# Mixer GEMMs in a seven-product form with four operand sums a side and chained PSUM copies, and x0 normalised ahead of the statistics of x1

## The chip, the cores and the metric

The kernel runs on one core of one Trainium2 chip. The metric is the device time of one execution in microseconds (us), median of the timed runs; lower is better. Three kinds of number appear below and should not be mixed. The *time* of a run (about 578.7 us) covers the whole execution. The *span* (about 577 us) is what the profile of one execution shows from its first to its last instruction. A *start time* such as 236.00 is counted from the beginning of that span.

## The reference, cut to what matters

```python
# A_x [1, 2048, 1024], A_wqkv [1024, 3072], A_wo [1024, 1024]; B_w1 [2048, 3584], B_w2 [3584, 2048]; all bf16
x = A_x
h = x + linear_attention(_layernorm(x), A_wqkv, A_wo)     # 32 heads, phi(t) = elu(t) + 1
def _B_ref(x, w1, b1, w2, b2):                            # the token mixer
    h = _layernorm(x, axis=-1)
    u = jnp.einsum("bsd,sf->bdf", h, w1) + b1             # GEMM 1, contraction over S = 2048
    u = _gelu(u)
    y = jnp.einsum("bdf,fs->bds", u, w2) + b2             # GEMM 2, contraction over F = 3584
    return y.transpose(0, 2, 1)
return h + _B_ref(_layernorm(h), ...)
```

The two mixer GEMMs take 338 of the 577 us. The rest is the first layer norm, the projections, the linear attention, the output projection and the second layer norm.

## The kernel before

The mixer treats each GEMM as a 2x2 block product and does it with seven half-size products in place of eight. GEMM 1 runs 14 "pairs" (two tiles of 128 output rows), with 8 matmuls of 128x512 a product; GEMM 2 runs 8 pairs with 14 matmuls a product. In the class for this, `asum` makes the weight-side operand sums on VectorE, `combine` makes the sums of the moving side on VectorE, and `mK` issues product K and whatever must be done with its result in PSUM.

```python
class Strassen:                       # cut
    self.sa = {3: self.a11, 4: self.a22}
    def asum(self, m):                # five weight-side sums a pair, each on VectorE
        a, b, op = {
            1: (self.a11, self.a22, ALU.add),
            2: (self.a21, self.a22, ALU.add),
            5: (self.a11, self.a12, ALU.add),
            6: (self.a21, self.a11, ALU.subtract),
            7: (self.a12, self.a22, ALU.subtract),
        }[m]
        ...
        return nc.vector.tensor_tensor(t, a, b, op)
    def m2(self, ks=None):            # W = product 2, and a copy of it to SBUF on ScalarE
        ...
        nc.scalar.copy(self.s2[:], self.W[:])
    def m3(self, ks=None):            # Z = product 3;  d = Z - s2                   VectorE
        ...
    def m1(self, ks=None):            # X = product 1;  Y = X + d                    VectorE
        ...
    def m4(self):                     # W += product 4; t = W + d                    VectorE
        ...
    def m5(self, cut=None):           # Z += product 5; t = t - Z;  X = X + t        VectorE, twice
        ...
    def m6(self): ...                 # Y += product 6, evacuate
    def m7(self): ...                 # X += product 7, evacuate (issued within the next pair)
```

The order of a pair in the steady part, and that of the first pair of GEMM 1 (`split`). There the last of the eight matmuls of three products is held back, because the last two row tiles of the layer norm are still being made:

```python
def run_pair(st, nxt, split, pending, cut=None):
    if split:
        for ks in (head, last):
            st.m2(ks); st.m3(ks); st.m1(ks)
        st.m4()
    else:
        st.m2()
        if pending is not None:
            pending.m7()
        st.m3(); st.m4(); st.m1()
    ...  # nxt.asum(2)
    st.m5(cut)
    ...  # nxt.asum(1), nxt.asum(5)
    st.m6()
    ...  # nxt.asum(6), nxt.asum(7)
```

The start of the kernel. `pin` holds an instruction in the written order on its engine. `ln[1][1](c)` is the statistics of half c of row tile x1 (VectorE), `norm_halves(0)` the normalising of x0 (VectorE), and `transpose_in(0)` its eight transposes on TensorE and the copies out of PSUM:

```python
warm_up(10)                     # matmuls on a scratch tile, so that the clock is up
...
ln_stats(0)                     # statistics of x0, VectorE
stats(0)                        # scale of x0: Ln and Exp on ScalarE
ln[1] = ln_chunks(1, xs.pop(1))
pin(ln[1][1](0))                # first half of x1's statistics, VectorE
norm_halves(0)
transpose_in(0)
pin(ln[1][1](1))
pin(ln[1][2]())
stats(1)
k_unit(0, 0)                    # first projection
```

## Time and profile before

| what | measured |
|---|---|
| time, median of 3 runs | 578.66 us (578.49 to 578.73) |
| span of the profile | 577.5 us |
| busy TensorE / VectorE / ScalarE | 569.7 / 385.8 / 212.9 us |
| first mixer matmul starts | 236.00 us |
| last matmul starts | 574.41 us |

In the profile PE is TensorE (matmuls), PEld its weight loads, DVE is VectorE, ACT ScalarE, SPq the queue that issues DMAs. The first view is the line of busy time in the page of the kernel before (busy us, share of the span, instructions):

```profile
PE 569.7 (99%) x2832; PEld 267.3 (46%) x2854; DVE 385.8 (67%) x752; ACT 212.9 (37%) x433; POOL 1.8 (0%) x8
```

A busy matmul engine proves little by itself, because matmuls overlap (each is recorded as 0.379 us long, and the next starts 0.216 us after it) and their ends are modelled. What counts is the pitch from start to start, and whether there are gaps. The next view cuts the mixer of the kernel before into its two GEMMs, and shows for each stretch its length and the busy time and instructions of each engine:

```profile
core 0: us, PE busy (x) PEld busy (x) DVE busy (x) ACT busy (x) POOL busy (x), PEclk, DMA share, GB/s
236.00:406.10 170.10, 170.10 (x790) 77.11 (x789) 115.04 (x204) 48.71 (x75) 0.00 (x0) 1.00 0.30 81
406.10:574.50 168.40, 168.40 (x795) 77.07 (x793) 91.01 (x114) 5.39 (x9) 0.00 (x0) 1.00 0.41 115
```

TensorE is busy for the whole of both stretches. VectorE is busy for two thirds of the first and half of the second and never holds TensorE up. In the chain of work that ended last, one product of eight matmuls takes 1.73 us, so 0.216 us for each matmul (the piece is a whole product of the first pair):

```profile
241.78 1.73 PE psW L228 x8
```

The third view is the timeline of the start of the kernel before (start us, us, engine, line, operation, output <- inputs, shapes, count; in brackets the engine's idle time before it and what ended it):

```profile
3.59 1.29 DVE L396 BATCH_NORM_STATS2 st<-x_sb 128x6 f32<-128x512 bf16 x2 [1.49 <-DMA x_sb<-in_A_x_dram]
...
5.49 0.20 ACT L403 ACTIVATE rstd<-lnv 128x1 f32<-128x1 f32 x1
5.84 0.69 DVE L396 BATCH_NORM_STATS2 st<-x_sb 128x6 f32<-128x512 bf16 x1 [0.72 <-DMA x_sb<-in_A_x_dram]
6.45 0.72 DVE L406 TENSOR_SCALAR xn<-x_sb,mv,rstd 128x512 bf16<-128x512 bf16 x2
...
6.91 0.72 PE L670 MATMUL tp<-ident,xn 128*128 128x128 bf16 x8 [1.26 <-DVE xn L406]
```

The scale of x0 (`rstd`) is ready at 5.69 us, the end of the ACTIVATE. VectorE then does a half of x1's statistics, normalises x0 from 6.45 on, and x0's transposes start at 6.91.

### The profile page before, as it was taken

The page shows a single profiled execution, that of the slowest core. Times are in us where ns is not written, and L with a number is a line of the kernel's source. Part 1 is how long each engine was busy: PE and PEld are TensorE (multiplying, and loading weights), DVE is VectorE, ACT ScalarE, POOL GpSimd, SP SyncE. Part 2 cuts the span into 40 slices and gives each one's busy share as a digit, 9 for nine tenths or more (in the row PEclk, how much of TensorE's full clock was granted, in tenths as well). Part 3 has the DMA queues.
Part 4 walks back from the last instruction along what each step waited for, and adds up shares of the span by engine and source line. Part 5 has one row for each costly group of instructions (what it writes and reads, how often), then busy time and mean ns, then how long its engine had stood idle before and what let it go on. Part 6 is the DMA issues. An engine that isn't in the chain of part 4 may idle for free.

```text
span 577.5 us, 7489 instructions
## 1 busy us (share of the span) xinstructions
PE 569.7 (99%) x2832; PEld 267.3 (46%) x2854; DVE 385.8 (67%) x752; ACT 212.9 (37%) x433; POOL 1.8 (0%) x8
## 2 busy tenths in 40 slices
PE   7999999999999999999999999999999999999997
PEld 3444444455555444444444444444444444444444
DVE  6898887556767889876756766667765455456443
ACT  4747777656668777332222322223000000000000
POOL 1000000000000000000000000000000000000000
PEclk9999999999999999999999999999999999999999
DMA  9934431039438952152224322203966446431101
GB/s 304 350 75 77 90 73 37 19 116 273 68 73 176 279 165 92 63 139 73 74 75 122 95 74 73 74 0 95 227 207 161 127 114 173 133 96 47 36 28 36
DMA packets 109827, 66.55 MB, mean 115 GB/s; under 512 B 31826, under 2 KB 101728, under 8 KB 109792
## 3 DMA queue, kind: packets, MB, share of 16 engines
q1 hardware_dynamic: 109056, 65.42, 42.3%
q10 hardware_dynamic: 672, 0.66, 0.4%
q8 instruction: 22, 0.36, 0.3%
q14 instruction: 13, 0.11, 0.1%
q0 software_dynamic: 64, 0.01, 0.0%
HBM read 50.34 MB, written 8.39 MB: 102 GB/s over the span
## 4 chain that ended last, share of the span: by engine, by line
PE 95%; DVE 2%; DMA 1%; issue 1%; SPq 0%; ACT 0%
PE psW L228 17%; PE psZ L228 17%; PE psX L228 17%; PE acc_t L922 10%; PE acc_t L775 9%; PE psY L228 8%; PE psB L503 4%; PE psC L503 4%; PE psA L503 4%; PE psE L503 2%; PE acc_t L427 1%; DMA x_sb<-in_A_x_dram 1%; PE nd_ps L873 1%; DVE wo_sb L477 1%; DVE st L396 0%
## 5 line engine op out<-in xcount | busy, mean ns | idle before, releaser
L228 PEld LDWEIGHTS <-sa 128*128 128x128 f16 x1134 | 110.4, 98 | 131.7
L223 DVE TENSOR_TENSOR sa<-w1p 128x1024 f16<-128x1024 bf16 x70 | 48.0, 686 | 20.0 <-PE psX L228 12.4
L775 PE MATMUL acc_t<-xnT,wq_sb 128*128 128x512 bf16 x248 | 57.3, 379 | 0.4
L922 PE MATMUL acc_t<-wo_sb,pqT 128*128 128x512 bf16 x250 | 55.7, 379 | 0.3
L223 DVE TENSOR_TENSOR sa<-w2p 128x1792 f16<-128x1792 bf16 x40 | 43.4, 1085 | 10.1 <-PE psW L228 7.6
L922 PEld LDWEIGHTS <-pqT 128*128 128x128 bf16 x256 | 24.8, 98 | 29.0
L775 PEld LDWEIGHTS <-wq_sb 128*128 128x128 bf16 x256 | 24.5, 98 | 27.4
L164 DVE TENSOR_SCALAR e_sb<-e_sb 128x512 bf16<-128x512 bf16 x64 | 18.5, 289 | 25.9 <-ACT e_sb L160 25.4
L264 DVE TENSOR_TENSOR tt<-psW,dd 128x512 f32<-128x512 f32 x22 | 15.2, 692 | 29.2 <-PE psW L228 29.2
L228 PEld LDWEIGHTS <-w2p 128*128 128x128 bf16 x224 | 21.9, 98 | 26.4
L228 PEld LDWEIGHTS <-w1p 128*128 128x128 bf16 x224 | 21.9, 98 | 26.4
L259 DVE TENSOR_TENSOR psY<-psX,dd 128x512 f32<-128x512 f32 x22 | 15.4, 700 | 27.5 <-PE psX L228 27.5
L160 ACT ACTIVATE e_sb<-acc_t 128x512 bf16<-128x512 f32 x40 | 23.9, 598 | 26.6 <-PE acc_t L775 23.6
L503 PEld LDWEIGHTS <-xs 128*128 128x128 f16 x208 | 20.1, 98 | 23.3 <-DVE xs L489 1.3
L269 DVE TENSOR_TENSOR tt<-tt,psZ 128x512 f32<-128x512 f32 x22 | 15.1, 688 | 18.0 <-PE psZ L228 17.9
L228 PE MATMUL psZ<-hT_2227,w1p 128*128 128x512 f16 x112 | 26.8, 379 | 0.0
L503 PE MATMUL psA<-wkv,xnT 128*128 128x512 bf16 x98 | 26.4, 379 | 0.3
L228 PE MATMUL psW<-hE,sa 128*128 128x512 f16 x112 | 26.6, 379 | 0.0
L228 PE MATMUL psX<-hT_2226,sa 128*128 128x512 f16 x112 | 26.6, 379 | 0.0
L228 PE MATMUL psX<-hO,sa 128*128 128x512 f16 x112 | 26.5, 379 | 0.0
L228 PE MATMUL psW<-hT_2228,w1p 128*128 128x512 f16 x112 | 26.5, 379 | 0.0
L228 PE MATMUL psZ<-hO,sa 128*128 128x512 f16 x112 | 26.5, 379 | 0.0
(258 smaller groups left out, 840.1 us busy)
## 6 DMA issues: line engine op xcount, KB each, us to landing
w1p<-in_B_w_dram SPq DMA_DIRECT2D x14, 1024.0 KB, 5.7
w2p<-in_B_w_dram SPq DMA_DIRECT2D x8, 1792.0 KB, 8.3
xr<-in_A_x_dram SPq DMA_DIRECT2D x16, 256.0 KB, 3.5
x_sb<-in_A_x_dram SPq DMA_DIRECT2D x15, 256.0 KB, 3.0
wkv<-in_A_wqkv_dram SPq DMA_DIRECT2D x2, 1024.0 KB, 9.2
wq_sb<-in_A_wqkv_dram SPq DMA_DIRECT2D x2, 1024.0 KB, 12.4
wo_sb<-in_A_wo_dram SPq DMA_DIRECT2D x2, 1024.0 KB, 6.4
wkv<-in_A_wqkv_dram SPq DMA_DIRECT2D x3, 512.0 KB, 7.5
```

Of the source, the lines that this page charges most:

```text
L160: pin(nc.scalar.activation(e_sb[:], src, ACT.Exp))
L164: pin(nc.vector.tensor_scalar(e_sb[:], e_sb[:], 1.0, PHI_EPS, ALU.min, ALU.add))
L223: return nc.vector.tensor_tensor(t, a, b, op)
L228: nc.tensor.matmul(ps[:, cols], lhsT=sa[:, k, :], rhs=mv(k)[:, cols], start=(start and k == 0), stop=(stop and k == self.nk - 1), skip_gro ...
L259: nc.vector.tensor_tensor(self.Y[:], self.X[:], self.d[:], ALU.add)
L264: nc.vector.tensor_tensor(self.t[:], self.W[:], self.d[:], ALU.add)
L269: nc.vector.tensor_tensor(self.t[:], self.t[:], self.Z[:], ALU.subtract)
L427: mm = nc.tensor.matmul(pp[:, 0:CW], lhsT=xnT[:, kt, i * P:(i + 1) * P], rhs=wkv[:, kt, c * CW:(c + 1) * CW], start=(kt == 0), stop=(kt == ...
L477: pin(nc.vector.tensor_tensor(out, a, b, ALU.subtract))
L503: pin(nc.tensor.matmul(ps[:], lhsT=lhs[:, k, :], rhs=rhs[:, k, :], start=(start and k == 0), stop=(k == hk2 - 1), skip_group_check=True,))
L775: nc.tensor.matmul(qp[:, 0:SW], lhsT=wq_sb[:, kt, j * P:(j + 1) * P], rhs=xnT[:, kt, u * SW:(u + 1) * SW], start=(kt == 0), stop=(kt == ND ...
L922: nc.tensor.matmul(ap_[:, 0:CW], lhsT=pqT[:, j, i * P:(i + 1) * P], rhs=wo_sb[:, j, dc * CW:(dc + 1) * CW], start=(j == 0 and not SEED_RES ...
```

## The change

The intent is to take work off VectorE. The same seven products a pair are combined in another way: four operand sums a side, some of them built on earlier ones, and accumulators that are chained by copies within PSUM on ScalarE (A to B, B to C), with one shared product E. The last pair of GEMM 1 also prepares the first weight sums of GEMM 2. At the start, x0 is normalised before any statistics of x1.

```diff
-    class Strassen:
+    class Product7:
...
+            self.lhs = {1: self.a11, 2: self.a12, 4: self.a22}
         def asum(self, m):
             a, b, op = {
-                1: (self.a11, self.a22, ALU.add),
-                2: (self.a21, self.a22, ALU.add),
-                5: (self.a11, self.a12, ALU.add),
-                6: (self.a21, self.a11, ALU.subtract),
-                7: (self.a12, self.a22, ALU.subtract),
+                5: (self.a21, self.a22, ALU.add),
+                6: (self.lhs.get(5), self.a11, ALU.subtract),
+                7: (self.a11, self.a21, ALU.subtract),
+                3: (self.a12, self.lhs.get(6), ALU.subtract),
             }[m]
...
+        def p1(self):
+            self.A = psw.tile([P, BANK], F32, tag="w", name="psA1")
+            self.mm(1, self.A, True)
+            self.B = psx.tile([P, BANK], F32, tag="x", name="psB1")
+            nc.scalar.copy(self.B[:], self.A[:])
+        def p5(self, ks=None):        # E = product 5, then shared(E)
+        def p6(self):
+            self.mm(6, self.B, False)
+            self.C = psy.tile([P, BANK], F32, tag="y", name="psC1")
+            nc.scalar.copy(self.C[:], self.B[:])
+        def p2(self, ks=None):        # A += product 2, evacuate
+        def p7(self, cut=None):       # C += product 7, evacuate with E added
+        def p3(self):                 # B += product 3, evacuate with E added
+        def p4(self):                 # C += product 4, evacuate (issued within the next pair)
...
-    def run_pair(st, nxt, split, pending, cut=None):
+    def run_pair(st, nxt, pending, cut=None):
+        st.p1()
+        if pending is None:           # first pair of a GEMM
+            head, last = list(range(st.nk - 1)), [st.nk - 1]
             for ks in (head, last):
+                st.p5(ks)
+                st.p2(ks)
         else:
+            pending.p4()
+            st.p5()
+        st.p6()
+        if pending is not None:
+            st.p2()
+        st.p7(cut)
+        st.p3()                       # asum 5, 6, 7, 3 of the next pair lie between; cut
...
             stats(0)
-            ln[1] = ln_chunks(1, xs.pop(1))
-            pin(ln[1][1](0))
             norm_halves(0)
             transpose_in(0)
-            pin(ln[1][1](1))
-            pin(ln[1][2]())
+            ln_stats(1)
             stats(1)
```

Below, "product 2" and "second product" mean the one with that number (`p2`), not the second in time.

## The prediction

> **What bounds it.** The matmul engine. By the page's first part PE is busy 569.7 of 577.5 us. Busy time alone proves little for pipelined matmuls (the Trainium skill, "Perfetto Trace Analysis", section Identifying the Most-Contended Engine), so I read the pitch. In the chain of waits the mixer is one string of products: 8 matmuls per 1.73 us, 14 per 3.02 us, 0.216 us for a 128x512 matmul. The skill's "TensorE: Matmul & The Clock Gate", section "Wait — 56ns, not 53.3ns?", states 215.7 ns for back-to-back warm ones; the trace agrees. Cut into windows, PE was busy 170.1 of 170.1 us in the first mixer GEMM (236.0 to 406.1) and 168.5 of 168.9 in the second. Most idle PE lies in the first 11 us (1.2 before the warm-up, then 1.3, 0.4, 0.5) and 2.5 us of tail.
>
> **Mixer.** Both forms do seven products per pair with 8 or 14 matmuls each: the same count, so nothing to gain on PE. The load falls elsewhere:
> - VectorE, first GEMM, per pair of 12.1 us: 5 operand sums at 0.69 become 4; 5 PSUM combinations at 0.69 become 2; four 0.42 sums become 3: about 8.6 us becomes 5.4. Second GEMM, per pair of 21.2 us: 5x1.08+5x0.69+4x0.75 = 11.9 becomes 4x1.08+2x0.69+4x0.75 = 8.7.
> - ScalarE: one 0.59 us copy becomes three (two in the second GEMM).
> Off the critical path: worth about 0.
>
> New waits could cost. A product started on a PSUM copy waits for it: 0.2 us until ScalarE sees the last matmul, 0.57 of copy, some 0.05 to PE: 0.85. In the steady order a whole product stands between (1.73 or 3.02), which hides it. In the first pair of each GEMM the built order puts only 5 or 4 matmuls (1.08, 0.86) of the next pair between; in the first GEMM the copy also queues behind the Gelu table load (1.28) and a Gelu (0.69). I give 0 to 0.2 us.
>
> At the hand-over the loads of weight pairs 1 and 2 of the second GEMM now start when the last fourth product ends (406.1), where the first started at 398.5. At the 290 GB/s of those loads before, each takes 6.3 us, and the residual rows behind land near 421.5. VectorE stands still for them, but PE needs its evacuation only at the fourth product, near 427: 2.5 us to spare. This is the thinnest place.
>
> **Start.** Before, after x0's scale was ready (5.69), VectorE did the first statistics of x1 (5.84 to 6.53), and normalising began at 6.45. Now it begins near 5.75: x0's transposes and first projection move 0.7 us ahead. x1's statistics end no later, so x1's transposes, which waited for PE until 9.72, start some 0.4 us earlier. After that PE is continuous to 14.25, and x3's input (landed 12.48) still meets its turn. About 0.35 us should survive to the end.
>
> **Time.** 578.66 - 0.35 + 0.1 of new waits = 578.4 us, 8 in 10 between 577.6 and 579.6. Faster by over 2%: 0.005; within 2%: 0.985; slower: 0.01.
>
> **Right or wrong by.** First transposes near 6.2 instead of 6.9; first mixer matmul near 235.6; mixer windows wholly PE-busy at 0.216 us; VectorE busy down from 386 to about 312, ScalarE up from 213 to about 235; VectorE's long wait for residual rows within 414 to 422, no PE gap after it.
>
> **What would make it wrong.** Residual rows landing after 424 (up to a few us, once); ScalarE's queue order delaying a copy in every pair (0.1 us times 22 would show); the early 0.35 lost to a later DMA landing.

## The result, and the profile after

The changed kernel took 579.02 us (median of 6 runs, 578.84 to 579.42); the kernel before, in runs on the same chip, 578.69 us (6 runs, 578.49 to 580.43). A ratio here is the mean time of one kernel's runs over that of the other's of the same rounds, so it is not quite the ratio of these medians. (Every run here counts, the long ones described below too.) It is 0.9998 (95% interval 0.9983 to 1.0013): the same within 2%, in fact within 0.2%. Both profiled spans are 577.5 us.

The line of busy time in the page of the changed kernel:

```profile
PE 570.2 (99%) x2832; PEld 267.5 (46%) x2854; DVE 323.6 (56%) x641; ACT 234.0 (41%) x470; POOL 1.8 (0%) x8
```

VectorE lost 62 us of work and ScalarE gained 21, with the same number of matmuls. The mixer of the changed kernel in windows, cut at its own hand-over:

```profile
core 0: us, PE busy (x) PEld busy (x) DVE busy (x) ACT busy (x) POOL busy (x), PEclk, DMA share, GB/s
235.57:405.19 169.62, 169.48 (x786) 76.69 (x784) 77.45 (x134) 65.42 (x103) 0.00 (x0) 1.00 0.26 70
405.19:574.50 169.31, 169.31 (x799) 77.48 (x797) 68.02 (x81) 10.06 (x18) 0.00 (x0) 1.00 0.45 125
```

The first stretch has 0.14 us in which TensorE was not busy. Because the ends of matmuls are modelled, I measured gaps from start to start instead: the time by which a matmul starts later than the pitch after the one ahead of it. The kernel before has none above 0.03 us in the whole mixer. The changed kernel has exactly two, both in the first pair of GEMM 1: **0.112 us** before 238.92 and **0.302 us** before 243.96. Its timeline of that pair:

```profile
237.29 1.67 PE L208 MATMUL psE_2922<-hE,sa 128*128 128x512 f16 x7
...
237.85 0.30 ACT L951 ACTIVATE hln_l<-mv_all,eps_85 128x1 f32<-128x1 f32 x1 [1.01 <-DVE mv_all L949]
238.18 0.20 ACT L952 ACTIVATE sc_all<-hln_l 128x1 f32<-128x1 f32 x1
238.29 0.58 ACT L224 COPY psB_2920<-psA_2911 128x512 f32<-128x512 f32 x1
...
238.92 1.67 PE L208 MATMUL psA_2911<-hO,w1p 128*128 128x512 f16 x7
...
240.86 1.89 PE L208 MATMUL psB_2920<-hT_2226,sa 128*128 128x512 f16 x8
241.44 1.28 ACT L272 ACT_TABLE_LOAD   x1
...
242.58 1.24 PE L208 MATMUL psA_2984<-hE,w1p 128*128 128x512 f16 x5
242.74 0.69 ACT L272 ACTIVATE gE<-psA_2911,b_sb 128x512 f16<-128x512 f32 x1
...
243.32 0.59 ACT L236 COPY psC_2952<-psB_2920 128x512 f32<-128x512 f32 x1
...
243.96 0.81 PE L208 MATMUL psC_2952<-hT_2227,sa 128*128 128x512 f16 x3
```

The first gap: product 2 adds to accumulator A (238.92), so the copy from A to B must have *read* A first. That copy, at 238.29, stands in ScalarE's queue behind the scale of the last layer norm (237.85 and 238.18), which itself waited for VectorE. The second gap: product 7 adds to C (243.96), and the copy from B to C stands behind the load of the Gelu table (1.28 us) and the first Gelu (0.69 us). The Trainium skill, "PSUM — Partial Sum Buffer", section Engine vs sequencer instructions, states that the ScalarE queue is a strict first-in, first-out one. The trace agrees: product 6 ended near 242.6 and the copy, due some 0.2 us later, started only at 243.32, while the Gelu ahead of it was finishing.

The timeline of the start of the changed kernel, which answers to that of before:

```profile
5.57 0.20 ACT L421 ACTIVATE rstd<-lnv 128x1 f32<-128x1 f32 x1
5.81 0.74 DVE L424 TENSOR_SCALAR xn<-x_sb,mv,rstd 128x512 bf16<-128x512 bf16 x2 [0.60 <-ACT rstd L421]
6.28 0.95 PE L688 MATMUL tp<-ident,xn 128*128 128x128 bf16 x8 [0.64 <-DVE xn L424]
6.46 1.28 DVE L414 BATCH_NORM_STATS2 st<-x_sb 128x6 f32<-128x512 bf16 x2
```

The transposes started at 6.28 in place of 6.91, and the mixer began at 235.57 in place of 236.00. Put together for these two profiles:

| | before | after | difference |
|---|---|---|---|
| first mixer matmul starts | 236.00 | 235.57 | -0.43 |
| from there to the last matmul's start | 338.41 | 338.82 | +0.41 |
| last matmul starts | 574.41 | 574.39 | -0.02 |

So in these two traces a start that is 0.43 us earlier pays for two new waits of 0.41 us. That is a complete account of the pair of profiles. The experiments ask whether it is also the account of the *kernels*.

Two theories stood at the outset. The first: the start is worth 0.4 us in every execution, the new combination costs 0.4 us, and they cancel. The rival: one of the two terms is particular to these executions. A second rival, for the mixer, said that the relief of VectorE is worth something and is eaten by copies all along the mixer, and not by two waits in one pair.

### The profile page after: what moved, and what is told of

Read it like the earlier page. It is cut to its first block, busy times and chain, and to the rows that moved or that the text cites. A ratio compares the mean times of both kernels' runs of the same rounds, so it can differ in the third digit from the quotient of the medians.

```text
span 577.5 us, 7392 instructions
## 1 busy us (share of the span) xinstructions
PE 570.2 (99%) x2832; PEld 267.5 (46%) x2854; DVE 323.6 (56%) x641; ACT 234.0 (41%) x470; POOL 1.8 (0%) x8
## 4 chain that ended last, share of the span: by engine, by line
PE 94%; DMA 2%; ACT 2%; DVE 2%; issue 1%; SPq 0%; ACTq 0%
PE acc_t L937 10%; PE acc_t L790 9%; PE psB L521 4%; PE psC L521 4%; PE psA L521 4%; PE psE L521 2%; PE nd_ps L888 1%; DMA xr<-in_A_x_dram 1%; PE psC_4189 L208 1%; PE psB_5038 L208 1%; PE psA_5023 L208 1%; PE psC_4961 L208 1%; PE psC_4831 L208 1%; PE psB_4778 L208 1%; PE psB_4648 L208 1%; PE psA_4633 L208 1%
## 5 line engine op out<-in xcount | busy, mean ns | idle before, releaser
L208 PEld LDWEIGHTS <-sa 128*128 128x128 f16 x896 | 87.7, 98 | 106.0 <-issue 0.4
L200 DVE TENSOR_TENSOR sa<-w1p 128x1024 f16<-128x1024 bf16 x28 | 19.1, 684 | 13.7 <-PE psB_2920 L208 1.2
L948 DVE BATCH_NORM_STATS2 hst<-acc_t 128x6 f32<-128x512 f32 x32 | 22.1, 692 | 6.9 <-ACT h_bf L947 6.5
L935 ACT CAST acc_t<-xr 128x512 f32<-128x512 bf16 x32 | 19.0, 593 | 13.5 <-DVE hst L948 13.4
L161 ACT ACTIVATE r_sb<-acc_t 128x512 bf16<-128x512 f32 x40 | 23.7, 593 | 0.0
L200 DVE TENSOR_TENSOR sa<-w2p 128x1792 f16<-128x1792 bf16 x16 | 17.4, 1088 | 9.8 <-DMA w2p<-in_B_w_dram 3.0
L909 DVE TENSOR_TENSOR o_sb<-nd_ps,rd 128x384 bf16<-128x384 f32 (+1 forms) x48 | 21.7, 504 | 1.0 <-ACT rd L904 0.8
L445 PE MATMUL acc_t<-wkv,xnT 128*128 128x512 bf16 x94 | 21.1, 379 | 0.9 <-ACT xnT L698 0.8
L414 DVE BATCH_NORM_STATS2 st<-x_sb 128x6 f32<-128x512 bf16 x32 | 20.4, 681 | 1.6 <-DMA x_sb<-in_A_x_dram 1.6
L947 ACT CAST h_bf<-acc_t 128x512 bf16<-128x512 f32 x32 | 18.3, 574 | 1.2 <-PE acc_t L937 1.1
```

The source lines that it names most:

```text
L161: pin(nc.scalar.activation(r_sb[:], src, ACT.Relu))
L208: nc.tensor.matmul(ps[:, cols], lhsT=lhs[:, k, :], rhs=mv(k)[:, cols], start=(start and k == 0), stop=(k == self.nk - 1), skip_group_check ...
L414: return nc.vector.bn_stats(st[:, c, :], x_sb[:, c * CW:(c + 1) * CW])
L445: mm = nc.tensor.matmul(pp[:, 0:CW], lhsT=xnT[:, kt, i * P:(i + 1) * P], rhs=wkv[:, kt, c * CW:(c + 1) * CW], start=(kt == 0), stop=(kt == ...
L909: nc.vector.tensor_tensor(o_sb[:, b * JPB * P:(b * JPB + nsl) * P].rearrange("p (s h e) -> p s h e", h=HB, e=DH), blk[:, :, 0:P].rearrange ...
L935: nc.scalar.copy(ap_[:, 0:CW], xr[:, dc * CW:(dc + 1) * CW])
```

## The experiments

Every kernel below gave the reference's result. Twelve kernels were run beside runs of the kernel before. Some executions are about 1.7 us longer, nearly all of these with a recorded clock of 0.997 in place of 1.0 or 0.999. I call those *long* and the others *undisturbed*; what a long one is comes out under e5 and e9.

### e1_start_only: the kernel before with the new start

```diff
 stats(0)
-ln[1] = ln_chunks(1, xs.pop(1))
-pin(ln[1][1](0))
 norm_halves(0)
 transpose_in(0)
-pin(ln[1][1](1))
-pin(ln[1][2]())
+ln_stats(1)
 stats(1)
```

> The kernel before with the new start order alone. Theory (the start gains 0.43 us and keeps it; the new GEMM form loses 0.41 us in its first pair): first mixer matmul at 235.57 instead of 236.00, no gap in the mixer, last matmul at 573.98 instead of 574.41, span 577.1. Rival (the start's gain is swallowed later, as by a DMA landing, and the GEMMs cost nothing): last matmul at 574.4, span 577.5.

Measured: 578.62 us (578.45 to 578.82, 6 runs), ratio 0.9992 (0.9979 to 1.0005), span 576.7. The mixer began at 235.21 and took 338.41 with no gap.

The mixer is as it was. Neither theory's figures came out: its last matmul started at 573.61, where 573.98 or 574.4 was expected. And the six runs do not separate from the undisturbed runs of the kernel before: 27 undisturbed runs of it have a median of 578.64. The mixer began 0.8 us earlier than in the profile of before, and yet the time is no shorter than that of its ordinary executions.

### e2_gemms_only: the changed kernel with the old start

The edit is the reverse of the one above, in the changed kernel.

> The changed kernel with the old start order. Theory: first mixer matmul at 236.00; two gaps on the matmul engine in the first pair, 0.11 and 0.30 us; last matmul at 574.82, span 577.9. Rival (the GEMM form costs nothing by itself): last matmul at 574.4, span 577.5.

Measured: 579.04 us (578.83 to 581.53, 6 runs, one of them long), ratio 1.0006 (0.9988 to 1.0024), span 577.3. Two gaps, 0.114 and 0.302 us, and 338.83 from the first mixer matmul to the last. The mixer began at 235.32, earlier than with the *new* start in the profile after. The timeline of the start of e2 shows why:

```profile
5.09 0.64 DVE L414 BATCH_NORM_STATS2 st<-x_sb 128x6 f32<-128x512 bf16 x1
...
5.54 0.20 ACT L421 ACTIVATE rstd<-lnv 128x1 f32<-128x1 f32 x1
5.77 0.73 DVE L424 TENSOR_SCALAR xn<-x_sb,mv,rstd 128x512 bf16<-128x512 bf16 x2
6.24 0.72 PE L688 MATMUL tp<-ident,xn 128*128 128x128 bf16 x8 [0.60 <-DVE xn L424]
```

This is the old order, and it costs nothing. Here x1 had landed in time, so its first statistics ran from 5.09 to 5.73, inside the time in which VectorE had to wait for the scale (5.74) anyhow. In the profile of before, x1 landed at 5.82, 4.6 us after its issue. In the eleven other profiles with x1's load in its place it took 2.9 to 3.7 us and landed at 4.1 to 4.9. So that one profile caught an uncommon execution.

The four combinations of start and GEMM, medians of undisturbed runs:

| | GEMMs of before | GEMMs of after |
|---|---|---|
| old start | 578.64 (27 runs) | 579.03 (5 runs of e2) |
| new start | 578.62 (6 runs of e1) | 579.02 (6 runs) |

Down a column the start is worth 0.01 to 0.02. Along a row the GEMMs cost 0.39 and 0.40, what the two gaps add up to in the traces. (The runs come from several chips, so I read this as agreement to about 0.1 us, no more.)

### e3_table_early, e4_copy_first, e5_both: take the waits away one at a time

e3 fetches the Gelu table early, with one Gelu of a single column right after the first product and its copy; e4 puts the first copy ahead of the last layer norm's scale in ScalarE's queue; e5 does both. All three start from the changed kernel.

```diff
 st.p1()
+if pending is None and st.nk == NSP:                                           # e3, e5
+    pin(nc.scalar.activation(g_dummy[:], eps_ln[:], ACT.Gelu_apprx_tanh))
...
-    nc.scalar.copy(self.B[:], self.A[:])
+    first_copy = nc.scalar.copy(self.B[:], self.A[:])                          # e4, e5
+    # the last layer norm's Ln on ScalarE is ordered after first_copy
```

In e5 the small Gelu is also ordered after the last layer norm's scale, so that the table changes once.

> The changed kernel with the Gelu table fetched by a dummy activation right after the first pair's first PSUM copy. Theory (the second gap, 0.30 us, is the copy queued behind the table load and one Gelu): that gap goes to 0.00, the first gap of 0.11 stays, mixer first to last matmul 338.5. Rival (the copy itself takes longer than the five matmuls in between): the gap of 0.30 stays, 338.8.

Measured for e3: 578.55 us in a single run, span 576.8. One gap, 0.111 us; the mixer takes 338.52. In the timeline of e3 the copy from B to C had nothing ahead of it and waited for product 6 alone:

```profile
242.35 0.57 ACT L237 COPY psC<-psB 128x512 f32<-128x512 f32 x1 [0.77 <-PE psB L209]
```

> The changed kernel with only the first pair's first PSUM copy put ahead of the last layer norm's two small activations on ScalarE. Theory (the first gap is the second product waiting for that copy to have read its bank, and the copy waiting in ScalarE's queue): gap of 0.11 goes to 0.00, the 0.30 one stays or grows to at most 0.41, since it hangs on the end of the second product plus table load and Gelu. Rival (the gap is weight loading or the matmul engine's own issue): 0.11 stays.

Measured for e4: 578.53 us in a single run, span 576.8. One gap, 0.302 us; the mixer takes 338.71. In the timeline of e4 the copy from A to B waited for product 1 alone:

```profile
236.85 0.57 ACT L225 COPY psB<-psA 128x512 f32<-128x512 f32 x1 [0.68 <-PE psA L209]
```

> The changed kernel with ScalarE's queue mended in the first pair: the first PSUM copy ahead of the last layer norm's two small activations, and the Gelu table fetched by a dummy activation right after them. Theory: both gaps close (0.00 to 0.05 us left), mixer's first to last matmul 338.4 instead of 338.8, last matmul at 573.98, span 577.1, about 0.4 us under both kernels; in the timed runs that is 0.07%, at the edge of what they resolve. Rival (the gaps are the copies' own latency): nothing changes, 577.5.

Measured for e5: 578.51 us (578.43 to 580.41, 6 runs), ratio 0.9992 (0.9977 to 1.0007). No gap in the mixer, which takes 338.41 as in the kernel before.

Each gap goes away when, and only when, its own cause does, and together they are the whole of the mixer's 0.41. (e5 against the changed kernel is 0.5 us by the times and 0.41 by the traces; they ran on different chips.)

The profile of e5 happened to catch a long execution, so it shows what one is. The windows of e5:

```profile
core 0: us, PE busy (x) PEld busy (x) DVE busy (x) ACT busy (x) POOL busy (x), PEclk, DMA share, GB/s
4.20:7.60 3.40, 1.69 (x13) 0.74 (x12) 2.77 (x7) 1.33 (x4) 0.00 (x0) 1.00 1.09 368
7.60:11.00 3.40, 3.40 (x12) 1.38 (x11) 2.54 (x7) 0.74 (x3) 0.00 (x0) 0.50 1.09 354
```

The column PEclk is 0.50 in the second line: from 7.60 to 11.01 TensorE ran at half clock. Half of 3.41 us of work is 1.7 us, the excess of the long executions. Note that e5 has the new start, and that x1 had landed in time (4.79): a long execution does not need a late x1. In e5 TensorE stood idle for 1.35 us between its warm-up and x0's transposes.

### e6_unhide: product 7 straight after product 6

```diff
+st.p7(cut)
 if pending is not None:
     st.p2()
-st.p7(cut)
```

All mixer matmuls are pinned in this order, in the changed kernel. Then nothing stands between a copy and the product that waits for it.

> The changed kernel with the seventh product straight after the sixth in every pair, and all mixer matmuls kept in that order, so that nothing stands between the copy's bank being finished and its use. Theory (a PSUM copy costs 0.88 us from last matmul to next: 0.26 to start, 0.57 copy, 0.05 to PE, and one product in between hides it): a gap of 0.85 to 0.90 in each of 21 pairs, 1.3 to 1.4 in the first pair of the first GEMM, in sum 19 us, so about 598 us. Rival (the matmul engine's queue or the next weights hide the copy anyway): under 3 us.

Measured: 597.21 us (597.04 to 597.49, 4 runs), ratio 1.0306 (1.0285 to 1.0328). The mixer took 357.16, which is 18.75 more than without gaps: 0.079 and 1.381 in the first pair, 0.821 in each of 19 pairs, 0.877 in each of the first two of GEMM 2. A pair in the steady part, from the timeline of e6:

```profile
277.80 1.89 PE L208 MATMUL psB<-hT,sa 128*128 128x512 f16 x8
...
279.73 0.57 ACT L236 COPY psC<-psB 128x512 f32<-128x512 f32 x1 [1.09 <-PE psB L208]
...
280.35 1.02 PE L208 MATMUL psC<-hT,sa 128*128 128x512 f16 x4 [0.66 <-ACT psC L236]
```

So a bare copy within PSUM between two products costs 0.82 us (the estimate in the prediction was 0.85), and the 1.73 or 3.02 us of the product in between hide it wholly in the changed kernel. The rival that put a cost on every pair falls.

### e7_vector_back: give VectorE its work back

```diff
 nxt.asum(7)
+nxt.again(7)          # the same sum into the same tile, as spare work
+nxt.again(7)
 st.p3()
 nxt.asum(3)
+nxt.again(3)
```

> The changed kernel with three operand sums of each pair done again (twice the seventh, once the third): some 2.1 us more VectorE work per pair of the first GEMM and 3.2 of the second, which gives back two thirds and all of what the change took away. Theory (VectorE's relief is off the critical path): VectorE busy up from 324 to about 375 us, no new gap over 0.05 us, time as the changed kernel. Rival (the relief gains something that the copies' cost hides): about 0.4 us or more slower, gaps before products that use a sum.

Measured: 578.93 us (578.77 to 579.21), ratio 0.9992 (0.9967 to 1.0017), and the same two gaps (0.104 and 0.303). The line of busy time in the page of e7:

```profile
PE 569.3 (99%) x2832; PEld 267.2 (46%) x2854; DVE 374.6 (65%) x704; ACT 233.9 (41%) x470; POOL 1.8 (0%) x8
```

VectorE does 51 us more than in the changed kernel (323.6), of the 62 that the change took away, and nothing changes: 578.93 against 579.02. The relief of VectorE is worth nothing that these runs can show.

### e8_late_rows: the spare time at the hand-over between the GEMMs

The prediction called the hand-over the thinnest place: the residual rows of GEMM 2's first pair are loaded behind two large weight loads, and VectorE stands still for them. In the changed kernel its timeline there reads

```profile
420.43 0.69 DVE L302 TENSOR_TENSOR e_4166<-psE_4138,hr_4115 128x512 f32<-128x512 f32 x1 [1.86 <-DMA hr_4115<-h_dram_97]
...
422.48 0.75 DVE L306 SCALAR_TENSOR_TENSOR ot_4120<-psC_4189,b_sb,e_4168 128x512 bf16<-128x512 f32 x1
...
426.35 1.03 PE L208 MATMUL psC_4189<-gT_4110,w2p 128*128 128x512 f16 x4
```

C is evacuated at 423.23 and needed at 426.35: 3.1 us to spare, 2.5 predicted. e8 loads one weight pair twice and puts the rows behind it.

```diff
 load_w2_pair(1, w2b)
 load_w2_pair(2, w2b)
+again = nc.sync.dma_start(w2_tiles[2][:], ...)      # the same pair once more
+# the first residual rows are ordered behind it on the queue
```

> The changed kernel with the weights of the second GEMM's pair 2 loaded twice, the residual rows behind that second load: the rows land about 8 us later, near 429. Theory (the only thing that hangs on the rows is VectorE's evacuation before pair 0's fourth product, with about 3.1 us to spare): one gap of 4.5 to 6.5 us before that fourth product (5.4 worked out), none elsewhere, time up by the same. Rival (the rows gate nothing that the matmul engine needs): no gap.

Measured: 583.99 us (582.86 to 584.26), ratio 1.0074 (1.0051 to 1.0097). One new gap, 3.45 us, before product 4, where 4.5 to 6.5 was expected. The timeline of e8:

```profile
427.81 1.09 DVE L200 TENSOR_TENSOR sa<-w2p 128x1792 f16<-128x1792 bf16 x1 [5.62 <-DMA w2p<-in_B_w_dram]
...
430.68 0.74 DVE L311 SCALAR_TENSOR_TENSOR ot<-psC,b_sb,e 128x512 bf16<-128x512 f32 x1
...
431.47 1.01 PE L208 MATMUL psC<-gT,w2p 128*128 128x512 f16 x2 [3.29 <-DVE ot L311]
```

The chain ends as named: VectorE, evacuation of C, product 4. But what ended VectorE's wait of 5.62 us was the second load of the weights (landed at 427.72), because the build had put a sum of those weights ahead; the rows landed at 428.39, while that sum ran. So e8 made both late, and by these times the rows alone would have held VectorE some 0.4 us less. Product 4 would have been up at 426.08. The build moved nine matmuls of the next pair (1.94 us) into the hole, and 3.45 + 1.94 = 5.4 us is its whole delay. Counted from the first mixer matmul, C was evacuated 8.5 us later than in the changed kernel and product 4 started 5.4 us later: the 3.1 us between them is the spare time. After the hole TensorE ran at half clock for 3.41 us, at a cost of some 1.6 us; the quickest run, at 582.86, may be one without it (it recorded a clock of 1.0, the other three 0.996). The spare time is real, and in the changed kernel it is not used up.

### e9_late_x1_old and e10_late_x1_new: make x1 late on purpose

Both have the GEMMs of before; e9 has the old start, e10 the new one. In both, x1's load is queued behind a 512 KB weight load.

```diff
 xs = {0: load_x(0, True)}
-xs[1] = load_x(1)
 pin(nc.scalar.dma_start(wkv[:, 0:hk, 0:CW], ...))
 nc.sync.dma_start(wkv[:, hk:ND, 0:CW], ...)
+xs[1] = load_x(1)
```

> The kernel before with x1's load put behind 512 KB of weights, so that x1 lands near 5.9 us in every execution. New theory of the start (the old order costs only when x1 lands later than about 5.1, when VectorE would have been waiting for x0's scale anyway; the profile of before caught such an execution at 5.82): normalising x0 waits for x1's first statistics, first transposes 1.2 to 1.5 us after x0's scale is ready instead of 0.50, last matmul 0.6 to 0.9 us later than the twin with the new order. The matmul engine idles over 1.2 us after its warm-up, so I also expect more executions with the clock halved for one stretch in the start (1.7 us longer): 2 or more of 6. Rival (the order of the start never matters): as the twin.

Measured for e9: 582.84 us (581.95 to 583.41), ratio 1.0067 (1.0049 to 1.0084). x1 landed at 7.28, later than I had meant (5.9). Its timeline and its windows:

```profile
5.17 0.20 ACT L403 ACTIVATE rstd<-lnv 128x1 f32<-128x1 f32 x1
7.28 0.69 DVE L396 BATCH_NORM_STATS2 st<-x_sb 128x6 f32<-128x512 bf16 x1 [2.47 <-DMA x_sb<-in_A_x_dram]
...
8.34 0.75 PE L670 MATMUL tp<-ident,xn 128*128 128x128 bf16 x8 [2.71 <-DVE xn L406]
```

```profile
5.50:8.90 3.40, 0.69 (x9) 0.45 (x8) 1.62 (x4) 0.12 (x1) 0.00 (x0) 1.00 1.08 368
8.90:12.30 3.40, 3.08 (x10) 1.01 (x8) 2.47 (x7) 1.35 (x4) 0.00 (x0) 0.50 1.08 364
```

The scale of x0 was ready at 5.37, and its transposes waited for *x1* until 8.34. TensorE then stood idle for so long that its clock was halved in the next stretch; five of the six runs recorded a clock of 0.997 or below. In the profiles of e9 and e10 the last matmuls start 2.6 us apart, and not the 0.6 to 0.9 expected for x1 at 5.9.

> The same late x1 with the new start order. New theory: first transposes 0.50 us after x0's scale is ready, whatever x1 does; undisturbed executions as those of the run with the start change alone (578.4 to 578.9), so 0.6 to 0.9 us under the twin with the old order; at most 1 of 6 with the halved clock. Rival: as the twin.

Measured for e10: 580.01 us (579.44 to 580.75), ratio 1.0018 (1.0002 to 1.0034); one of six runs was long. None of the six lies within the 578.4 to 578.9 that were expected. The timeline of e10:

```profile
5.47 0.74 DVE L406 TENSOR_SCALAR xn<-x_sb,mv,rstd 128x512 bf16<-128x512 bf16 x2 [0.60 <-ACT rstd L403]
5.94 0.72 PE L670 MATMUL tp<-ident,xn 128*128 128x128 bf16 x8 [0.30 <-DVE xn L406]
```

With the new order the transposes start 0.51 us after the scale (5.43), as if x1 were not late. So the new start does one real thing, which it was not predicted to do: it takes x0 out of reach of x1's DMA. With x1 this late e10 is 2.8 us shorter than e9, of which some 1.7 is the halved clock that e9 has in most runs. e10 is still 1.4 us longer than e1: x1's own transposes must wait for x1, and start at 9.92 in place of 8.93.

### e11_both_again and e12_more_warm: the version without gaps, timed again, and with a longer warm-up

e11 is the same kernel as e5. e12 is e5 with twelve warm-up matmuls in place of ten, in case the long executions could be warded off that way.

> The mended kernel again, for more executions. Theory (in ordinary executions the start change is worth 0 and the mended GEMMs cost 0): undisturbed executions within 0.15 us of the undisturbed ones of the kernel before, at most 1 of 6 with the halved clock.

Measured for e11: 578.37 us (578.28 to 578.64, 6 runs, none long), ratio 0.9991 (0.9976 to 1.0005), span 576.5, no gap, 338.41. The timeline of its first pair, which answers to that of the changed kernel:

```profile
236.89 0.57 ACT L227 COPY psB<-psA 128x512 f32<-128x512 f32 x1 [0.66 <-PE psA L211]
...
237.92 1.28 ACT L343 ACT_TABLE_LOAD   x1
...
238.20 1.67 PE L211 MATMUL psA<-hO,w1p 128*128 128x512 f16 x7
...
242.07 0.57 ACT L245 COPY psC<-psB 128x512 f32<-128x512 f32 x1 [0.77 <-PE psB L211]
```

Both copies now start 0.2 us after the product they read, with no other work ahead of them, and the table load has moved out from between them.

> The mended kernel with 12 warm-up matmuls instead of 10, which fills 0.4 us (full clock) to 0.9 us (half clock) of the matmul engine's wait for x0. If that wait is what lets the clock be halved in the start: 0 of 6 such executions; where the warm-up runs at half clock to its end (6.5 us) it delays x0's transposes by up to 0.3 us, so undisturbed executions 0 to 0.3 us longer than the mended kernel.

Measured for e12: 578.69 us (578.31 to 579.03), ratio 0.9995 (0.9980 to 1.0010), none long. It is 0.3 us slower than e11 on the same chip: in its profile the longer warm-up kept TensorE from x0's transposes until 6.29, 0.95 us after the scale in place of 0.51. With no long run in either, it tells nothing about long runs.

e11 has the lowest time of the kernels tried. Undisturbed runs of e5 and e11 together have a median of 578.44 (11 runs), 0.2 us under the kernel before. That is a tie by the ratio's interval, which holds 1.

### Why the ratio says 0.9998 when the undisturbed medians say +0.4

Undisturbed, the changed kernel is 0.4 us slower than the one before (579.02 against 578.64). The means behind the ratio are 579.08 and 579.20, because two of the six runs of the kernel before were long; that the ratio came out at 1 is luck. Counted by their time, over 580 us, over all timed runs with x1's load in its place (e8 left out, because it stalls for another reason): 9 of 41 runs with the old start were long, and 1 of 40 with the new one. (Two of the nine have no clock on record, and one, of 580.27, recorded 1.0.) The exact test of a 2x2 table gives a probability of about 0.008 for so many by chance on the side of the old start, 0.014 on either side; the question was put after the runs had been seen, so this is weaker than the number looks. The mechanism was forced in e9 and did not come in e10 but once. Still, no profile of an ordinary long execution of the kernel before was caught, and the one ordinary long execution that was caught, e5, had x1 in time. That late x1 causes those of the kernel before is suggested and not shown.

## Why the prediction was right or wrong, point by point

The time was right: 578.4 predicted, within 577.6 to 579.6, and 579.02 measured, with the class "within 2%". Some of it was right for its reasons. Two terms were wrong, and both erred to the low side: 0.35 us of gain that does not exist and 0.3 us of cost left out make up the miss of 0.6. A range of 2 us had room for both, so that it held says little about either. What cancelled were not the two errors but the two effects in the two spans of 577.5: a real cost of 0.41, and a gain of 0.43 over an execution of the kernel before that was uncommon.

**Right: TensorE bounds the kernel, and VectorE's relief is worth about 0.** The matmul count is unchanged, the pitch stayed 0.216 us, and the mixer stayed full but for 0.41 us. VectorE fell to 323.6 us (312 predicted, so 62 of the 74 us forecast), ScalarE rose to 234.0 (235 predicted). e7 gave VectorE 51 us back at no cost that shows.

**Right: copies in the steady order are hidden.** e6 removed the product that hides them and each cost 0.82 us (0.85 predicted), 18.75 us in sum. In the changed kernel none of these shows.

**Right: the hand-over holds.** 3.1 us to spare (2.5 predicted), with the rows at 420.4 (421.5 predicted). e8 showed that the chain named is the one that would break.

**Wrong in size: "I give 0 to 0.2 us" for new waits, entered in the sum as 0.1.** It is 0.41 us. The larger part, 0.302, is the wait that the prediction did name (the copy behind the Gelu table load and a Gelu in the first pair), but it gave it too little: by the estimate in the prediction itself, 1.08 us of the next pair's matmuls cannot cover 0.85 of copy *and* what is left of 1.28 + 0.69 ahead of it in the queue. e3 took away that gap alone. The other 0.112 was not foreseen at all. I had looked for who waits for the copy's *result*, and missed that product 2, which adds to the copy's *source*, must wait until the copy has read it. e4 took away that gap alone.

**Wrong: "About 0.35 us should survive to the end" from the start.** In the two profiles the gain is there, 0.43. In ordinary executions it is 0: e1 against before, and the changed kernel against e2, differ by 0.01 to 0.02 us. The start times that the prediction named came out (transposes at 6.28, 6.2 predicted; first mixer matmul at 235.57, 235.6 predicted), but by luck: the gain they stand for is over that one profile. The failed step is the reading of the timeline of before, "VectorE did the first statistics of x1 (5.84 to 6.53), and normalising began at 6.45", as the kernel's order at work. The bracket on that line said that VectorE had been waiting 0.72 us for a DMA. With x1 in time, the statistics fit in the wait for the scale, as e2 shows. The profiled execution also took 579.32 us, 0.7 more than the median of its timed runs, a second sign that it was not an ordinary one. The 0.43 can be split exactly by measuring from the moment the scale of x0 is ready to the first mixer matmul. That is 230.31 us in before's profile, 229.80 in after's and 229.58 to 229.66 in eight profiles of the experiments that were undisturbed up to there (e1, e2, e3, e4, e6, e7, e8, e11), whichever start they have. So before's profile lost about 0.7 to the late x1; after's lost 0.2, because its clock rose only at 7.01 and its eight transposes took 0.95 us in place of 0.72; and its scale was 0.08 later (5.77 against 5.69). 0.51 - 0.08 = 0.43. (The prediction had named a way for its 0.35 to be lost, a later DMA landing; it was not lost later, it was never there in ordinary executions.)

**What stays open.** Whether the long executions of the kernel before come from a late x1, as told above, and what makes one where x1 is in time, as in e5. And why x1's load took 4.6 us in that one profile was not looked into.

## What to carry to other kernels

When accumulators are chained by copies, look at both ends of each copy: the product that adds to its result and the product that adds to its source. Look also at what stands ahead of it in its engine's queue in the first iteration, where table loads and the tail of the stage before lie. Before counting a gain read from one profile, check that the wait it removes is in the kernel's order and not in that execution: if the bracket says that a DMA ended the wait, compare that DMA's landing time in other profiles, and the profiled run's own time with the median. Equal times can hide two effects that cancel, so time the parts apart (here a 2x2 of start and GEMM) and compare undisturbed runs before trusting the sum.

## What the Trainium skill lacked or had wrong

- "TensorE: Matmul & The Clock Gate", Part 1: The HAM clock gate (the "warmup" mystery), states a free-running window of 3413 ns, a clock at either half or full rate, and a fall to half rate after at least one idle window. The halved stretches here, 3.41 us at 0.50, agree with the length and the half rate, and the clock's first rise, at 4.0 to 7.0 us in the different profiles, fits a window that runs freely. The third, taken alone, is too narrow: in e5 the clock was halved after a 3.40 us stretch in which TensorE was busy for 1.69 us, far from idle. After a stretch of 3.41 us with 1.79 us busy, in the profile of before, it was not. The boundary in these traces lies near half the stretch being busy (the edges of a stretch that was not followed by a halving are inferred from when the clock rose, so this is an estimate).
- "ScalarE: Activation LUTs", What ACT_TABLE_LOAD costs, gives about 1283 ns for the load and about 1380 ns of drain, 2.66 us for each switch. The load agrees (1.28 us), but no drain shows in the trace of the changed kernel: the copy ahead ended at 241.42, the load started at 241.44 and the Gelu behind it at 242.74, 1.30 us later.
- No page that I looked up prices an accumulator handed from one matmul group to the next by a ScalarE copy within PSUM. Here a 128x512 f32 copy took 0.57 us, and TensorE lost 0.82 us where nothing was put in between (e6), which is about 4 matmuls of 128x512.
